# Normalized attention and a gated feed-forward layer: more work open to VectorE, the 1/6 at the end, and another written-out order

## The chip, the cores and the metric

One core of a Trainium2 chip runs the kernel as one program. The metric is the device time in microseconds, 425.38 as the median of three runs of the kernel before.

## The reference

```python
q, k, v: (8, 12, 448, 64)          # batch, heads, sequence, head size, float32
q_n = q / sqrt(mean(q * q) + 1e-6) * g_q;  k_n likewise with g_k
attn = softmax(q_n @ k_n.T / sqrt(64))
x = (attn @ v) as 3584 tokens x 768
h = x @ w_in                        # 768 -> 2048
g = h * clip(h + 3, 0, 6) / 6
out = g @ w_out                     # 2048 -> 768, float32
```

## The kernel before

The work goes by pairs of heads: pair P is batch P // 6 and two of its twelve heads, 48 pairs in all. For a pair, SyncE's queue loads queries, keys and values as tiles of 112 rows (four tokens to a row). Squares (`sq`, for half of a pair's queries `sqh`) are taken on ScalarE or GpSimd, VectorE sums them (`red`), ScalarE makes the inverse root from a logarithm and an exponential (`ln`, `ex`), and a scaling writes bf16 (`sc`, half: `sch`). For pairs 0 to 12 TensorE transposes the scaled tiles, and a copy takes them out of PSUM (`cq` for queries, `ck` for keys, which also multiplies by the gains); from pair 13 on a transposing DMA on SyncE's queue does it (`dt`), and `kt` applies the gains. Values are copied to bf16 (`cv`). Scores (`s`, on 64 of the array's 128 rows, two heads side by side) go to PSUM, ScalarE takes the exponential (`e`), TensorE multiplies with the values (`av`), VectorE divides (`rd`, `xn`), and the result is transposed into `xT`, by TensorE for the first two sequences and by DMA (`dx`) for the others.

The feed-forward part is split into groups: a hidden group (`h`) fills a PSUM bank with six matmuls, then the clamp (`relu`, line 726) and the product with h (`gate`, line 729) take it to `gT`; an output group (`y`) fills a bank with sixteen matmuls, copied out (`cy`) and stored. In the middle of the kernel these groups have two PSUM banks in turn. Attention of one sequence runs interleaved with feed-forward work of the one before it.

The first sequence is worked in halves, and short matmuls on zeros (`warm`, `idle`) fill TensorE in between. The weights come in by eight DMAs from GpSimd's queue.

Nothing of this is scheduled on the chip. `Plan.add` collects 2386 operations with the engines each may run on; `ORDER` is a written-out list of all their numbers in the order in which they are issued, and `WAY` says for an operation which of its allowed engines takes it (0, the first, where it isn't named). Each engine works its part strictly in that order, and so does SyncE's queue of loads, transposing DMAs and stores. Operation 369 is the load of the values of pair 12, 663 and 760 are the transposing DMAs of pairs 13 and 14.

The clamp and gate before:

```python
em(nc.scalar.activation(out=ts[:], in_=ps()[:, 0:S], func=RELU, bias=0.5, scale=1.0 / 6.0))
em(nc.vector.scalar_tensor_tensor(
    out=out, in0=shape(ts[:]), scalar=1.0, in1=shape(ps()[:, 0:S]), op0=A_MIN, op1=A_MULT))
```

Of the kernel before, what the change touches and what calls it, by code (L numbers as in the profile page):

```python
# [12 lines left out]
A_MIN = mybir.AluOpType.min  # L13
LN = mybir.ActivationFunctionType.Ln
# [9 lines left out]
    53: 1, 61: 1, 63: 2, 67: 1, 68: 1, 69: 1, 76: 1, 80: 1, 83: 1, 95: 1, 99: 1, 101: 2, 121: 1, 122: 1,  # L24
    126: 1, 128: 2, 148: 1, 199: 1, 212: 1, 214: 1, 232: 1, 346: 2, 386: 1, 387: 1, 393: 2, 457: 1, 462: 1,
    469: 1, 474: 1, 481: 1, 515: 1, 542: 1, 552: 1, 553: 1, 573: 1, 589: 2, 617: 1, 624: 1, 635: 1, 637: 1,
    646: 1, 653: 2, 664: 1, 672: 1, 737: 1, 738: 1, 769: 1, 770: 1, 776: 2, 795: 1, 802: 2, 854: 1, 926: 1,
    949: 1, 977: 1, 1005: 1, 1075: 1, 1134: 1, 1140: 2, 1160: 1, 1237: 1, 1269: 1, 1285: 1, 1286: 1, 1309:
    1, 1317: 1, 1318: 1, 1344: 1, 1350: 1, 1401: 1, 1408: 2, 1428: 1, 1434: 1, 1497: 1, 1565: 1, 1589: 1,
    1597: 1, 1615: 1, 1630: 2, 1641: 1, 1649: 1, 1673: 1, 1681: 1, 1688: 2, 1699: 1, 1707: 1, 1714: 2, 1725:  # L30
    1, 1785: 1, 1790: 1, 1817: 1, 1822: 1, 1857: 1, 1865: 1, 1872: 1, 1898: 2, 1941: 1, 1964: 1, 1979: 2,
    2039: 1, 2044: 1, 2072: 1, 2095: 1, 2114: 2, 2143: 1, 2151: 1, 2159: 1, 2195: 1, 2245: 1, 2286: 1, 2313:
    1, 2333: 1, 2338: 1, 2345: 1, 2357: 1, 2374: 1,
# [3 lines left out]
    9, 20, 8, 21, 22, 10, 23, 11, 24, 25, 13, 28, 26, 14, 27, 53, 16, 31, 55, 32, 17, 33, 54, 212, 12, 34,  # L37
    56, 213, 57, 29, 69, 92, 58, 61, 59, 19, 60, 35, 68, 73, 62, 36, 91, 30, 37, 74, 70, 214, 84, 66, 64,
    15, 75, 38, 67, 77, 65, 39, 71, 40, 118, 72, 83, 102, 76, 81, 119, 103, 104, 85, 41, 18, 79, 94, 95, 42,
    43, 93, 82, 80, 44, 215, 86, 230, 129, 96, 120, 87, 105, 45, 46, 89, 145, 47, 63, 97, 88, 130, 108, 146,  # L40
    131, 109, 110, 231, 111, 98, 132, 106, 99, 112, 113, 48, 100, 107, 216, 122, 114, 121, 133, 78, 115,
    158, 134, 232, 156, 149, 116, 217, 123, 49, 157, 50, 0, 135, 51, 136, 148, 117, 172, 233, 90, 124, 52,
    150, 125, 137, 159, 138, 127, 139, 164, 165, 126, 234, 140, 151, 235, 162, 152, 173, 174, 141, 154, 163,
    160, 142, 166, 153, 161, 175, 143, 167, 144, 188, 168, 101, 178, 189, 218, 176, 190, 179, 219, 177, 220,
    191, 180, 169, 200, 248, 242, 221, 181, 128, 201, 170, 155, 202, 225, 182, 249, 222, 236, 203, 183, 171,
    368, 223, 303, 184, 250, 192, 185, 245, 193, 304, 305, 339, 224, 186, 238, 194, 306, 187, 239, 315, 227,
    251, 340, 195, 204, 316, 246, 205, 196, 197, 317, 206, 237, 247, 341, 318, 207, 198, 360, 226, 240, 327,
    199, 329, 252, 208, 228, 342, 307, 253, 209, 308, 328, 271, 255, 241, 309, 147, 210, 310, 272, 211, 254,
    330, 243, 311, 347, 312, 273, 359, 319, 229, 320, 343, 256, 348, 321, 322, 257, 349, 323, 344, 313, 324,
    258, 350, 370, 314, 259, 325, 274, 1, 275, 371, 326, 331, 361, 372, 351, 373, 332, 333, 345, 374, 352,  # L50
    334, 375, 353, 362, 354, 335, 363, 397, 386, 355, 336, 364, 376, 263, 356, 398, 264, 377, 357, 337, 365,
    358, 399, 387, 338, 401, 378, 400, 265, 402, 276, 2, 388, 405, 500, 277, 379, 403, 501, 380, 489, 381,
    406, 404, 407, 408, 382, 389, 502, 409, 383, 506, 390, 3, 503, 410, 266, 384, 411, 385, 267, 507, 391,
    268, 412, 278, 504, 508, 505, 490, 512, 283, 513, 509, 346, 510, 392, 535, 491, 511, 284, 366, 514, 269,
    516, 525, 517, 515, 270, 518, 285, 519, 537, 492, 520, 524, 279, 493, 521, 536, 280, 286, 494, 522, 281,
    291, 523, 538, 495, 282, 539, 292, 526, 540, 541, 533, 287, 367, 545, 527, 293, 546, 543, 261, 528, 288,
    542, 544, 530, 260, 294, 547, 289, 548, 395, 566, 583, 549, 564, 290, 567, 299, 497, 550, 300, 529, 394,
    565, 393, 572, 244, 551, 301, 295, 554, 498, 573, 302, 296, 552, 262, 570, 582, 421, 297, 422, 571, 553,
    568, 298, 593, 5, 595, 569, 584, 423, 413, 414, 4, 424, 596, 574, 415, 555, 416, 417, 594, 425, 418,
    575, 576, 419, 577, 556, 426, 420, 557, 601, 585, 427, 559, 599, 578, 429, 602, 428, 430, 558, 579, 607,  # L60
    433, 431, 618, 617, 434, 432, 580, 435, 437, 496, 581, 646, 438, 560, 436, 600, 619, 6, 597, 441, 439,
    647, 605, 598, 608, 442, 606, 440, 630, 7, 443, 628, 603, 445, 444, 604, 648, 446, 586, 738, 609, 588,
    449, 447, 450, 620, 629, 448, 587, 610, 611, 631, 612, 634, 453, 613, 451, 614, 454, 635, 452, 636, 615,
    637, 458, 616, 621, 623, 632, 657, 659, 633, 459, 531, 658, 460, 622, 638, 660, 639, 455, 663, 640, 748,
    750, 749, 461, 591, 456, 532, 649, 751, 462, 561, 641, 470, 650, 642, 562, 651, 643, 664, 471, 625, 457,
    472, 652, 590, 644, 465, 645, 760, 737, 661, 754, 739, 756, 662, 466, 626, 769, 473, 796, 499, 740, 770,
    665, 534, 474, 666, 741, 755, 467, 743, 771, 746, 667, 795, 655, 668, 482, 742, 757, 669, 369, 670, 468,
    654, 821, 761, 671, 483, 786, 469, 672, 822, 772, 797, 780, 773, 782, 752, 781, 484, 396, 774, 823, 753,
    745, 477, 775, 478, 798, 783, 589, 758, 653, 812, 806, 853, 808, 759, 485, 762, 486, 804, 763, 764, 799,
    765, 777, 800, 809, 677, 766, 767, 479, 807, 880, 787, 768, 480, 854, 801, 678, 481, 624, 784, 855, 778,  # L70
    832, 879, 834, 785, 563, 673, 813, 824, 844, 674, 856, 679, 788, 825, 680, 675, 789, 826, 790, 835, 791,
    464, 685, 792, 827, 592, 793, 833, 686, 803, 676, 810, 744, 687, 840, 881, 838, 830, 857, 811, 681, 859,
    747, 682, 688, 861, 1017, 814, 683, 815, 794, 816, 841, 817, 684, 693, 858, 818, 839, 694, 819, 870,
    1018, 845, 866, 695, 836, 864, 867, 689, 696, 1049, 829, 776, 690, 865, 627, 1050, 701, 1019, 691, 820,
    702, 837, 692, 890, 892, 703, 802, 842, 463, 697, 1020, 843, 704, 896, 698, 1051, 882, 846, 699, 847,
    709, 476, 883, 891, 700, 848, 887, 849, 710, 1021, 893, 850, 888, 1023, 871, 705, 711, 851, 706, 884,
    1052, 712, 852, 1028, 707, 1030, 868, 885, 717, 708, 869, 862, 718, 1022, 1075, 872, 1040, 873, 719,
    874, 1031, 713, 720, 875, 1026, 1029, 714, 876, 886, 877, 725, 1076, 715, 878, 1034, 716, 894, 1035,
    726, 1101, 897, 721, 895, 1077, 1025, 828, 722, 727, 1102, 898, 899, 723, 900, 1134, 901, 724, 1133,
    1060, 1078, 1036, 1053, 902, 1061, 729, 903, 1055, 730, 728, 1037, 904, 1041, 1032, 731, 733, 1033, 734,  # L80
    732, 779, 1079, 1062, 1066, 735, 1038, 1081, 1086, 1039, 905, 736, 1103, 906, 1054, 656, 1042, 907,
    1057, 909, 1063, 1159, 908, 1043, 1092, 910, 913, 1024, 911, 1044, 912, 914, 860, 1135, 1045, 915, 917,
    1080, 1087, 918, 1046, 916, 1136, 1124, 919, 1067, 922, 1047, 923, 1058, 1093, 475, 1088, 1064, 1112,
    1084, 1065, 924, 889, 925, 1089, 1048, 1068, 926, 1160, 920, 1104, 1113, 1069, 488, 1070, 1071, 921,
    805, 1114, 1072, 1118, 1137, 1073, 1105, 929, 1115, 1139, 1110, 1161, 930, 1083, 1119, 1107, 933, 1109,
    1125, 931, 934, 831, 1106, 932, 1120, 935, 1090, 1144, 1162, 1318, 937, 936, 1138, 1091, 938, 1056,
    1167, 941, 1285, 942, 1141, 939, 1286, 1094, 863, 940, 1095, 1096, 1317, 1150, 1097, 945, 943, 1098,
    1099, 1163, 1121, 946, 1165, 944, 1142, 947, 1319, 1074, 1164, 950, 1146, 1287, 1116, 1100, 951, 1117,
    952, 1288, 1320, 1145, 1294, 948, 1168, 1147, 953, 949, 1059, 1170, 1289, 954, 1122, 1291, 928, 1172,
    1123, 957, 1027, 958, 1370, 487, 1126, 959, 1127, 1343, 1128, 1171, 1129, 961, 1130, 960, 1290, 962,  # L90
    1131, 965, 963, 1151, 1369, 966, 964, 1148, 967, 1082, 1296, 969, 1149, 968, 1111, 970, 1344, 1176,
# [865 lines left out]
```

## Time and profile before

| | |
|---|---|
| median of 3 runs | 425.38 us (425.29 to 426.16) |
| the profiled execution | 425.55 us, its span 423.8 us |
| TensorE busy | 414.8 us, 98% of the span |
| ScalarE busy | 287.1 us, 68% |
| VectorE busy | 225.8 us, 53% |
| GpSimd busy | 178.1 us, 42% |
| TensorE's granted clock | 0.998 |

The busy time of TensorE counts matmuls whose ends are modelled, so it says where TensorE has work and not that it runs at its peak. The other engines are far from full over the whole span, but not in every stage; the profile has to be read by stages. In the profile's names ACT is ScalarE, DVE VectorE, POOL GpSimd, SP SyncE, PE TensorE; a q behind a name is that engine's issuing queue.

### The profile page before, as it was taken

To read this page: it belongs to the slowest core of one execution; us is meant where nothing else is said; L and a number is where in the kernel's file an instruction comes from. 1 tells how busy PE (TensorE), PEld (TensorE's weight loads), DVE (VectorE), ACT (ScalarE), POOL (GpSimd) and SP (SyncE) were. 2 spreads that over 40 slices of the span, in tenths; PEclk is the share of its full clock that TensorE was granted. 3 is DMA by queue.
4 is the path that set the end of the run, shared out by engine and by line. 5 is a ranking of instruction groups with operands and counts; after the bars stand their busy time and mean duration, and the time that the engine had idled before them with its cause. 6 is when DMAs were issued, how large, how long until landed. Compare 5 with 4: busy or idle time off the path is not lost.

```text
span 423.8 us, 9991 instructions
## 1 busy us (share of the span) xinstructions
PE 414.8 (98%) x3960; PEld 243.0 (57%) x3960; DVE 225.8 (53%) x453; ACT 287.1 (68%) x523; POOL 178.1 (42%) x206
## 2 busy tenths in 40 slices
PE   7999999989999999999999999999999999999996
PEld 3566877645555555555555555555555555555564
DVE  5988774769775476565445455543453433232310
ACT  6999988789987768787767867666846662133101
POOL 3999685678774462593035655333030200000000
PEclk9999999999999999999999999999999999999999
DMA  7999999999869958595768469273144202200323
GB/s 249 292 282 220 244 216 170 274 267 274 207 155 267 249 129 226 172 197 144 198 154 239 110 159 215 79 184 77 40 106 112 57 26 60 43 7 0 109 68 118
DMA packets 98931, 67.77 MB, mean 160 GB/s; under 512 B 53156, under 2 KB 95428, under 8 KB 98884
## 3 DMA queue, kind: packets, MB, share of 16 engines
q1 hardware_dynamic: 93248, 60.50, 54.6%
q0 software_dynamic: 5248, 6.29, 9.0%
q8 instruction: 31, 0.51, 0.5%
q10 hardware_dynamic: 388, 0.34, 0.3%
q14 instruction: 16, 0.13, 0.1%
HBM read 50.23 MB, written 11.01 MB: 145 GB/s over the span
## 4 chain that ended last, share of the span: by engine, by line
PE 84%; DMA 6%; ACT 4%; issue 1%; DVE 1%; SPq 1%; POOL 1%; DVEq 0%; POOLq 0%; ACTq 0%
PE M L767 28%; PE M L789 27%; PE X L675 9%; PE S L589 5%; PE S L789 5%; PE X L589 3%; PE M L748 3%; DMA qk<-in_q_dram 3%; ACT eT L617 3%; DMA w_in_sb<-in_moe_w_in_dram 2%; DMA vf<-in_v_dram 1%; PE X L767 1%; PE S L767 1%; POOL qks L367 1%; PE X L789 1%
## 5 line engine op out<-in xcount | busy, mean ns | idle before, releaser
L367 POOL TENSOR_TENSOR qks<-qk,rs 112x512 bf16<-112x512 f32 (+1 forms) x88 | 88.9, 1024 | 119.5 <-ACT rs L428 94.8
L789 PE MATMUL M<-w_out_sb,gT 128*128 128x384 bf16 x752 | 138.0, 326 | 0.0
L767 PE MATMUL M<-xT,w_in_sb 128*128 128x448 bf16 x618 | 134.0, 353 | 0.0
L789 PEld LDWEIGHTS <-gT 128*128 128x128 bf16 x912 | 84.2, 98 | 58.3 <-issue 7.3
L729 DVE SCALAR_TENSOR_TENSOR gT<-ts,M 128x448 bf16<-128x448 f32 x119 | 73.3, 616 | 74.5 <-ACT ts L726 74.3
L595 ACT ACTIVATE eT<-S 112x896 bf16<-112x896 f32 x112 | 99.7, 916 | 6.9 <-PE X L675 3.6
L726 ACT ACTIVATE ts<-M 128x448 f32<-128x448 f32 x119 | 64.9, 546 | 46.5 <-PE M L767 39.4
L767 PEld LDWEIGHTS <-w_in_sb 128*128 128x128 bf16 x672 | 60.3, 98 | 58.2 <-issue 11.9
L364 POOL TENSOR_TENSOR sq<-qk 112x512 f32<-112x512 f32 (+1 forms) x59 | 59.1, 1012 | 24.1 <-DMA qk<-in_q_dram 9.6
L595 ACT ACTIVATE eT<-X 112x896 bf16<-112x896 f32 x56 | 51.3, 917 | 20.2 <-PE X L589 19.2
L675 PEld LDWEIGHTS <-eT 112*128 112x128 bf16 x1344 | 52.3, 97 | 15.1 <-DVE va L346 1.5
L675 PE MATMUL X<-va,eT 112*128 112x65 bf16 x1344 | 55.3, 193 | 1.4 <-DVE va L346 1.1
L449 DVE TENSOR_REDUCE ssq<-sq 112x16 f32<-112x1024 f32 x42 | 50.7, 1212 | 7.1 <-ACT sq L362 3.8
L589 PE MATMUL S<-T 64*128 64x448 bf16 x224 | 34.1, 353 | 0.1
L350 DVE COPY y<-M 128x384 f32<-128x384 f32 x23 | 12.8, 557 | 39.1 <-PE M L789 39.1
L694 DVE TENSOR_TENSOR xn<-X,rd 112x512 bf16<-112x512 f32 x42 | 28.9, 689 | 2.1 <-DMA xT<-xn 1.3
L691 DVE RECIPROCAL rd<-X 112x8 f32<-112x8 f32 x42 | 8.7, 207 | 38.2 <-PE X L675 35.4
L589 PEld LDWEIGHTS <-T 64*128 64x128 bf16 x336 | 12.3, 94 | 24.0 <-issue 18.8
L362 ACT ACTIVATE sq<-qk 112x512 f32<-112x512 f32 (+1 forms) x38 | 22.2, 595 | 5.6 <-DMA qk<-in_q_dram 3.4
L348 ACT COPY y<-M 128x384 f32<-128x384 f32 x24 | 11.5, 480 | 19.0 <-PE M L789 18.7
L748 PE MATMUL M<-xT,w_in_sb 128*128 128x224 bf16 x192 | 23.1, 259 | 0.2 <-DMA w_in_sb<-in_moe_w_in_dram 0.2
L789 PE MATMUL S<-w_out_sb,gT 128*128 128x384 bf16 (+1 forms) x128 | 22.3, 316 | 0.0
(88 smaller groups left out, 303.1 us busy)
## 6 DMA issues: line engine op xcount, KB each, us to landing
qk<-in_k_dram SPq DMA_DIRECT2D x45, 256.0 KB, 4.2
qk<-in_q_dram SPq DMA_DIRECT2D x45, 256.0 KB, 4.0
vf<-in_v_dram SPq DMA_DIRECT2D x45, 256.0 KB, 4.3
w_in_sb<-in_moe_w_in_dram POOLq DMA_DIRECT2D x4, 768.0 KB, 8.5
w_out_sb<-in_moe_w_out_dram POOLq DMA_DIRECT2D x4, 768.0 KB, 9.2
out_dram<-y SPq DMA_DIRECT2D x7, 336.0 KB, 3.9
out_dram<-y SPq DMA_DIRECT2D x8, 288.0 KB, 3.5
out_dram<-y SPq DMA_DIRECT2D x8, 240.0 KB, 2.7
```

The source lines that it names most:

```text
L364: em(nc.gpsimd.tensor_tensor(out=out, in0=in_, in1=in_, op=A_MULT))
L367: em((nc.vector if e == DVE else nc.gpsimd).tensor_tensor(out=out, in0=in_, in1=by.unsqueeze(3).to_broadcast(list(in_.shape)), op=A_MULT))
L449: em(nc.vector.tensor_reduce(out=ssq[:].rearrange("p i n -> p (i n)"), in_=sq[:].rearrange("p i (n d) -> p (i n) d", d=D), axis=AX_X, op=A ...
L589: em(nc.tensor.matmul(out=ps[:, a, 0:S], lhsT=qkT[r, S + t * TP:S + t * TP + 128], rhs=qkT[r, 0:S], start=True, stop=True))
L595: em(nc.scalar.activation(out=eT[:, t, 0:S2].rearrange("p (a s) -> p a s", a=2), in_=ps[0:TP, :, 0:S], func=EXP, bias=0.0, scale=1.0))
L675: em(nc.tensor.matmul(out=X_ps[:, a, i * E1:(i + 1) * E1], lhsT=eT[:, t, c:c + 128], rhs=va[:, a, t, :], start=(t == 0 and i == 0), stop=( ...
L694: em(nc.vector.tensor_tensor(out=xn[:].rearrange("p i a d -> p a i d"), in0=view()[:, :, :, 0:D], in1=rd[:].unsqueeze(3).to_broadcast([TP, ...
L726: em(nc.scalar.activation(out=ts[:], in_=ps()[:, 0:S], func=RELU, bias=0.5, scale=1.0 / 6.0))
L729: em(nc.vector.scalar_tensor_tensor(out=out, in0=shape(ts[:]), scalar=1.0, in1=shape(ps()[:, 0:S]), op0=A_MIN, op1=A_MULT))
L748: em(nc.tensor.matmul(out=ps()[:, f * SH:(f + 1) * SH], lhsT=w_in_sb[:, kt, f0:f0 + 128], rhs=xT[:, kt, z * SH:(z + 1) * SH], start=(kt == ...
L767: em(nc.tensor.matmul(out=ps()[:, 0:S], lhsT=w_in_sb[:, kt, f * 128:(f + 1) * 128], rhs=xT[:, kt, :], start=(kt == 0), stop=(kt == NKT - 1)))
L789: em(nc.tensor.matmul(out=ps()[:, 0:nc0], lhsT=gT[:, f, i * 128:(i + 1) * 128], rhs=w_out_sb[:, f, c0:c0 + nc0], start=(f == 0), stop=(f = ...
```

## The change

It has five parts. Squares may go to VectorE too for pairs below 15 (`NVE`), and scalings likewise. The clamp may go to VectorE for the first two sequences; to make that one instruction of two operations, ReLU(h + 3) is stored instead of ReLU(h/6 + 1/2), the gate clips at 6 instead of 1, and the missing 1/6 is applied in the copies of y. Value loads of the last three pairs are issued as two halves (`NSL`). `ORDER` and `WAY` are replaced altogether; the operations keep their numbers and what they depend on.

By engine, the new `WAY` moves 19 of the 128 clamps to VectorE; squares go from 57 on GpSimd and 33 on ScalarE to 48, 40 and 2 on VectorE; scalings from 4 on VectorE to 7, and one half scaling; value copies from 26 on GpSimd, 17 on VectorE, 5 on ScalarE to 18, 14 and 16; `kt` from 22 on VectorE and 13 on ScalarE to 20 and 15.

```diff
+    NSL = 3
+    NVE = 15
...
     def square(e, out, in_):
         if e == ACT:
             em(nc.scalar.square(out=out, in_=in_))
         else:
-            em(nc.gpsimd.tensor_tensor(out=out, in0=in_, in1=in_, op=A_MULT))
+            em((nc.vector if e == DVE else nc.gpsimd).tensor_tensor(out=out, in0=in_, in1=in_, op=A_MULT))
...
+            split = i == 2 and P >= NP - NSL
...
-                em(nc.sync.dma_start(out=dst, in_=rows))
+                for h in ((0, 1) if split else (slice(0, 2),)):
+                    em(nc.sync.dma_start(out=dst[:, h], in_=rows[:, h]))
...
-            plan.add("sq", [POOL, ACT], f_sq, ...
+            plan.add("sq", [POOL, ACT, DVE] if P < NVE else [POOL, ACT], f_sq, ...
...
-            plan.add("sc", [POOL], f_sc, ...
+            plan.add("sc", [POOL, DVE] if P < NVE else [POOL], f_sc, ...
...
-        def f_r(_):
-            em(nc.scalar.activation(out=ts[:], in_=ps()[:, 0:S], func=RELU, bias=0.5, scale=1.0 / 6.0))
+        def f_r(e):
+            if e == DVE:
+                em(nc.vector.tensor_scalar(ts[:], ps()[:, 0:S], 3.0, 0.0, A_ADD, A_MAX))
+            else:
+                em(nc.scalar.activation(out=ts[:], in_=ps()[:, 0:S], func=RELU, bias=3.0, scale=1.0))
...
-                out=out, in0=shape(ts[:]), scalar=1.0, in1=shape(ps()[:, 0:S]), op0=A_MIN, op1=A_MULT))
-        plan.add("relu", [ACT], f_r, [res], [("ts", key)])
+                out=out, in0=shape(ts[:]), scalar=6.0, in1=shape(ps()[:, 0:S]), op0=A_MIN, op1=A_MULT))
+        plan.add("relu", [ACT, DVE] if b < 2 else [ACT], f_r, [res], [("ts", key)])
...
-                copy(e, ys[:, c0:c0 + nc0], ps()[:, 0:nc0])
+                o, y = ys[:, c0:c0 + nc0], ps()[:, 0:nc0]
+                if e == ACT:
+                    em(nc.scalar.activation(out=o, in_=y, func=COPY, bias=0.0, scale=1.0 / 6.0))
+                else:
+                    em(nc.vector.tensor_scalar(o, y, 1.0 / 6.0, None, A_MULT))
```

The start of SyncE's queue behind operation 663 (k16: keys of pair 16; dt: transposing DMA of `T`), before and after:

```
before  dt(13) k17 q15 q16 k16 q18 q17 dt(14) k18 v14 v15 k20 k19 v12 q19 dt(15) v13 q20 dt(16)
after   dt(13) k16 v13 v15 q16 q17 k19 k17 k18 v12 k21 q19 q18 dt(14) q20 k20 v17 dt(15) v14 dt(16)
```

More of the change, by code (lines that the diff above doesn't have):

```diff
@@ L13 @@
 A_MIN = mybir.AluOpType.min
+A_MAX = mybir.AluOpType.max
 LN = mybir.ActivationFunctionType.Ln
@@ L415, in load, with fn @@
             dst = dst[0:np] if i == 2 else dst[0:np, i]
-            def fn(_, dst=dst, src=src, np=np):
+            split = i == 2 and P >= NP - NSL
+            def fn(_, dst=dst, src=src, np=np, split=split):
                 rows = src[b, hs].rearrange("h (p t) d -> p h (t d)", t=T)
                 rows = bass.AP(rows.tensor, rows.offset, [[rows.ap[0][0], np]] + [list(d) for d in rows.ap[1:]])
-                em(nc.sync.dma_start(out=dst, in_=rows))
+                for h in ((0, 1) if split else (slice(0, 2),)):
+                    em(nc.sync.dma_start(out=dst[:, h], in_=rows[:, h]))
             plan.add("ld", [SP], fn, (), [res] if i == 2 else [(*res, 1)] if i else [(*res, 0, z) for z in range(2)])
@@ L444, in f_sq @@
                 square(e, sq[:, i], qk[0:TP, i].rearrange("p h x -> p (h x)"))
-            plan.add("sq", [POOL, ACT], f_sq, [(*qr, 1)] if i else [(*qr, 0, z) for z in range(2)],
+            plan.add("sq", [POOL, ACT, DVE] if P < NVE else [POOL, ACT], f_sq, [(*qr, 1)] if i else [(*qr, 0, z) for z in range(2)],
                      [("sq", P % NSQ, 2)] if i else [("sq", P % NSQ, z) for z in range(2)])
@@ L459, in f_sc @@
                       qk[0:TP, i].rearrange("p h (t d) -> p h t d", d=D), rs[:, i].rearrange("p (h t) -> p h t", h=2))
-            plan.add("sc", [POOL], f_sc, ([(*qr, 1)] if i else [(*qr, 0, z) for z in range(2)]) + [wr[i]],
+            plan.add("sc", [POOL, DVE] if P < NVE else [POOL], f_sc, ([(*qr, 1)] if i else [(*qr, 0, z) for z in range(2)]) + [wr[i]],
                      [("qks", P % NQS, 2)] if i else [("qks", P % NQS, z) for z in range(2)])
@@ L469, in f_sq @@
                    qk[0:TP, 0, :, z * 2 * D:(z + 1) * 2 * D])
-        plan.add("sqh", [POOL, ACT], f_sq, [(*qr, 0, z)], [("sq", P % NSQ, z)])
+        plan.add("sqh", [POOL, ACT, DVE], f_sq, [(*qr, 0, z)], [("sq", P % NSQ, z)])
     def half_scale(P, z, rs, rr):
@@ L494, in f_sq @@
             square(e, sq[:, 8 * D:], qk[0:TP, 1].rearrange("p h x -> p (h x)"))
-        plan.add("sq", [POOL, ACT], f_sq, [(*qr, 1)], [("sq", P % NSQ, 2)])
+        plan.add("sq", [POOL, ACT, DVE], f_sq, [(*qr, 1)], [("sq", P % NSQ, 2)])
         half_square(P, 0)
```

281 rows, old and new, of tables (ORDER, WAY) are left out of this document.

## The prediction

> **What bounds the kernel now.** I read the busy time of each engine by stage first, then who waited for whom, then the chain of waits, and the single instructions last. By stage (columns: window, length, then busy us and count for matmul, weight load, VectorE, ScalarE, GpSimd, then TensorE's clock, DMA share, GB/s):
>
> ```profile
> 10.00:20.00 10.00, 9.18 (x124) 5.11 (x126) 9.68 (x25) 9.94 (x26) 8.55 (x12) 1.00 1.07 307
> 20.00:35.00 15.00, 14.55 (x261) 10.25 (x260) 12.70 (x42) 14.84 (x26) 14.21 (x19) 1.00 1.00 276
> 35.00:45.00 10.00, 9.58 (x140) 7.25 (x139) 7.93 (x18) 9.41 (x17) 9.88 (x12) 1.00 1.20 196
> ...
> 60.00:92.00 32.00, 30.92 (x341) 20.38 (x340) 19.46 (x36) 25.54 (x46) 20.39 (x23) 1.00 1.06 229
> 92.00:250.00 158.00, 158.00 (x1510) 87.41 (x1509) 95.24 (x174) 125.59 (x231) 84.39 (x91) 1.00 0.75 193
> 250.00:360.00 110.00, 110.00 (x1007) 61.86 (x1003) 48.49 (x96) 69.44 (x114) 27.33 (x29) 1.00 0.43 101
> ```
>
> From 92 to 360 us TensorE is never idle: no faster work elsewhere can be felt there. The set of TensorE's instructions is the same in both programs, so what can change is its idle time, nearly all before 92 us, and the price of its transitions. From 10 to 35 us ScalarE is the full one (9.94 of 10, 14.84 of 15), with VectorE (9.68) close behind. The waits of TensorE, in the first 45 us and from 45 to 360:
>
> ```profile
> PE M L537 <- POOL qks L367: 1.0, 1, 1.0
> ```
> ```profile
> PE X L675 <- DVE va L346: 1.1, 1, 1.1
> PE X L675 <- ACT eT L595: 0.3, 1, 0.3
> ```
>
> The one large wait behind the front is the 1.1 us for a copy of values. The chain of waits (start, us, what) tells whose it is:
>
> ```profile
> 75.98 2.06 POOL qks L367 x2
> ...
> 78.05 1.23 SPq L556
> ...
> 82.44 6.31 DMA vf<-in_v_dram
> ...
> 89.47 0.10 DVE va L346
> 89.57 0.05 issue
> 89.61 1.15 PE X L675 x32
> ```
>
> Two scalings on GpSimd release the transposing DMA of pair 14 (operation 760); it stands at the head of SyncE's queue, and behind it five loads and then the values of pair 12 (operation 369), issued at 82.44, landed 6.31 us later. VectorE copies them, and TensorE has waited.
>
> **The change, part by part.** *The value load, -1.1 us.* In the changed order operation 369 stands ahead of 760, eight loads behind the transposing DMA of pair 13 (operation 663), whose issue before was
>
> ```profile
> 72.75 1.34 SPq L556 DMA_TRANSPOSE T<-qks  x1
> ```
>
> Between 78.05 and 82.44 one transposing DMA and five loads took 1.23 us and 3.16 us, 0.63 each. With the same start: 72.75 + 1.34 + 8 x 0.63 = 79.1 us issued, with 6.31 to land 85.4, some 3 us before TensorE asks (89.61 - 1.1 = 88.5). The wait goes; what is late next behind it is a load whose place is new as well (a rival, below). Bounds: 1.1 gained, or nothing.
>
> *Score batches, -0.6 us.* Scores use half the rows of the array. The chain shows what entering and leaving them costs:
>
> ```profile
> 93.20 0.29 PE X L589 x2
> 93.49 0.38 PE S L589 x4
> 93.87 1.24 PE M L767 x6
> 95.11 0.97 PE X L675 x32
> 96.09 1.14 PE M L767 x6
> ```
>
> The first pair takes 0.29 us where each of the next two takes 0.19, and six matmuls behind scores take 1.24 where six others take 1.14: 0.2 us per batch. I counted unbroken batches in both built programs: 90 before, 87 after. 3 x 0.2 = 0.6 us, on TensorE itself.
>
> *The front, +0.5 us.* Single instructions of ScalarE, then one of GpSimd (start, us, what, idle before it):
>
> ```profile
> 6.88 0.42 ACT L362 ACTIVATE sq<-qk 112x256 f32<-112x256 f32 x1 [1.55 <-DMA qk<-in_q_dram]
> ...
> 9.35 0.62 ACT L362 ACTIVATE sq<-qk 112x512 f32<-112x512 f32 x1
> 9.87 0.90 ACT L617 ACTIVATE eT<-S 112x896 bf16<-112x896 f32 x1
> ...
> 10.97 0.62 ACT L356 ACTIVATE gT<-M,gp_t 128x448 bf16<-128x448 bf16 x1
> ```
> ```profile
> 10.66 1.04 POOL L364 TENSOR_TENSOR sq<-qk 112x512 f32<-112x512 f32 x1 [1.06 <-DMA qk<-in_k_dram]
> ```
>
> The third load lands at about 6.86, the eighth at about 10.6: 0.75 us each. The changed program squares the first keys on VectorE, but ScalarE's queue then holds, ahead of the copy of the scaled keys of pair 0, the squares of the third, fourth and fifth loads. The fifth lands at 6.86 + 2 x 0.75 = 8.4. Then a square (the next one starts 0.52 later: 9.35 to 9.87), the copy of the keys (row at 10.97; now ScalarE's, VectorE's before; 0.5 until the next starts), three short steps for roots and a half copy, some 0.7, its end and the scores, 0.5: the first exponential starts at about 10.6 us, not 9.87. That is 0.7 later on the engine that is full until 35 us. ScalarE's work from there to 35 us stays the same within a tenth: by the two orders a half square, a key copy and a half copy leave it, a whole square and a value copy come. VectorE's order in the first 35 us gains a square, a value copy, a half scaling, two copies and a whole scaling and loses a scaling, a value copy and a copy, about 1.1 us more in a stage in which it was 9.68 of 10 busy. Its free time of 2.3 us from 20 to 35 us can take that. Bounds: 0 (TensorE's fillers and ScalarE's 0.8 us free between 10 and 45 us take it up) and +1.8 (0.7 + 1.1, all passed on). I take 0.5, near the delay that ScalarE's rows give.
>
> *Clamps, 0.* Of 128, 19 move to VectorE, all before 121 us. Nothing before shows a clamp there; the nearest rows (mean ns last but one):
>
> ```profile
> L726 ACT ACTIVATE ts<-M 128x448 f32<-128x448 f32 x119 | 64.9, 546 | 46.5 <-PE M L767 39.4
> ```
> ```profile
> L729 DVE SCALAR_TENSOR_TENSOR gT<-ts,M 128x448 bf16<-128x448 f32 x119 | 73.3, 616 | 74.5 <-ACT ts L726 74.3
> L449 DVE TENSOR_REDUCE ssq<-sq 112x16 f32<-112x1024 f32 x42 | 50.7, 1212 | 7.1 <-ACT sq L362 3.8 <-POOL sq L364 3.3
> ...
> L367 DVE TENSOR_TENSOR qks<-qk,rs 112x512 bf16<-112x512 f32 x4 | 2.7, 687 | 0.2
> ```
>
> I take the gate's 616 ns, the same size from the same memory: 0.07 us more for each bank, and 19 x 0.62 = 11.8 us of work moved from ScalarE to VectorE, which has 12.5 us free from 60 to 92. ScalarE gets value copies and squares in exchange, so little is freed. What hides it is the other bank's group of six matmuls (1.14) with attention between; without that cover it is the first rival.
>
> *Squares and scalings, 0.* Two squares, three whole scalings more and a half one go to VectorE (687 ns for a scaling). They have a price on GpSimd:
>
> ```profile
> 13.97 1.06 POOL L367 TENSOR_TENSOR qks<-qk,rs 112x256 bf16<-112x256 f32 x1
> ```
> ```profile
> 13.87 0.69 DVE L367 TENSOR_TENSOR qks<-qk,rs 112x512 bf16<-112x512 f32 x1
> ```
> ```profile
> L367 POOL TENSOR_TENSOR qks<-qk,late_rs 112x256 bf16<-112x256 f32 x5 | 3.0, 613 | 0.0
> ```
>
> A half scaling that took 1.06 us on GpSimd instead of 0.61 began 0.1 us into a scaling on VectorE: 0.45 lost. Six more such instructions cost GpSimd up to 2.7 us. I count it as nothing, since GpSimd hands over nine squares and eight value copies. The Trainium skill ("SBUF — State Buffer", section "Who interferes with whom") says that a VectorE instruction with two SBUF inputs and a GpSimd one that reads SBUF exclude each other, and that the one issued first keeps the ports to its end; the row agrees, and by that rule VectorE can also be the one that waits. With 0.45 for each of the three in the first 40 us on the path, the sum would be 1.35 us higher.
>
> *The rest, 0.* The 1/6 in the copies of y replaces a copy by a scaling copy of the same size. The bounds are a tenth of a microsecond each way for one copy, off the path except for the last, after which the same store follows: the end is as long as it was. The split value loads of the last three pairs add three issues where TensorE waits for nothing (250 to 360 us).
>
> The profiled execution took 425.55 us: 425.55 - 1.1 - 0.6 + 0.5 = 424.35. The median of the runs is 425.38, 0.17 lower: **424.2 us**. About 0.2% (0.85 us) is what a measurement of this kernel can tell from no change.
>
> **The rivals.** *VectorE becomes the bound with the clamps (slower).* Clamp and gate now stand in one queue with the reductions of 1.21 us. A bank takes 2 x 0.62 = 1.24 us to empty, and 2.45 if a reduction is ahead; the other bank covers 1.14, attention in between about half a microsecond: 0.8 us of wait. It decides from the point where several clamps meet a reduction. Four of the 19 make 3.2 us: 424.2 + 3.2 = 427.4. For it: VectorE is 7.9 of 10 busy from 35 to 45 us, and the clamps between there and 60 us come on top. Against it: 12.5 us free from 60 to 92.
>
> *Another wait of a microsecond in place of the one removed (no change).* Every load has a new place, and one that lands late as pair 12's values did gives 424.2 + 1.1 = 425.3; the front at its full +1.8, or the ports' 1.35, gives 425.5 or 425.6. For it: DMA shares of about 1 until 92 us, and the values of pair 14 now behind one transposing DMA more. Against it: those of pairs 12, 13 and 15 stand earlier.
>
> *The front gets shorter (faster).* TensorE's idle time from 10 to 45 us is 0.82 + 0.45 + 0.42 = 1.7 us, and with the pair-0 queries scaled sooner the 1.0 us wait for GpSimd at 8.4 us goes. Without the 0.5 and with 1.0 less: 422.7.
>
> That the change does less than it says is built in: few instructions move, the order is what differs.
>
> **How the numbers follow.** Forecast 0.42, shorter front 0.10, another wait 0.20, VectorE bound 0.28. Faster is the first two, 0.52; same 0.20; slower 0.28. The forecast's own range is 423.7 (front at 0) to 424.7 (0.5 more). The range for all runs from 422.7 to the slow rival's 427.4; beyond lie a still shorter front and more than four clamps caught, under 2 in 10.
>
> **What would show it.** Right: no wait of TensorE for the value copies near 88 us, the first exponential at about 10.6 us, TensorE without idle time from 92 to 360 us. Wrong: waits of TensorE for VectorE's gate between 45 and 120 us (the slower rival), a new wait for a DMA, or a first exponential before 9.9 us.

## The result, and the profile after

The changed kernel takes 424.32 us as the median of 22 runs (422.91 to 425.56); the kernel before, run beside it, 425.78 us (22 runs, 423.86 to 427.79). The ratio is 0.9967 with a 95% interval of 0.9954 to 0.998: 1.4 us faster. The forecast was 424.2. The profiled execution took 424.31 us with a span of 422.5; that of before 425.55 and 423.8.

The stages after (columns as in the prediction):

```profile
10.00:20.00 10.00, 8.41 (x122) 5.40 (x123) 9.92 (x28) 9.97 (x25) 8.65 (x13) 1.00 1.10 333
20.00:35.00 15.00, 13.81 (x252) 9.91 (x252) 11.75 (x39) 13.80 (x25) 12.35 (x17) 1.00 1.03 267
...
60.00:92.00 32.00, 32.00 (x348) 20.81 (x346) 23.02 (x41) 25.16 (x48) 18.95 (x20) 1.00 1.11 242
92.00:250.00 158.00, 157.85 (x1516) 88.00 (x1514) 99.98 (x178) 127.11 (x229) 77.77 (x82) 1.00 0.82 194
250.00:360.00 110.00, 110.00 (x995) 62.04 (x994) 50.81 (x99) 70.35 (x117) 24.25 (x26) 1.00 0.42 93
```

From 60 to 92 us TensorE is now without idle time (32.00; before 30.92). In the front it has more: it works 8.41 us from 10 to 20 us against 9.18, and 13.81 from 20 to 35 us against 14.55. Over the first 92 us the idle time is 5.3 us in both profiles, so this pair alone does not show that the change won anything there; the runs have to. TensorE's waits after, the whole span:

```profile
PE XF L643 <- DVE xT L356: 0.9, 1, 0.9
PE S L621 <- ACT gT L354: 0.7, 1, 0.7
...
PE M L546 <- POOL qks L373: 0.4, 1, 0.4
PE M L760 <- DVE gT L741: 0.3, 1, 0.3
```

The wait for the values of pair 12 (1.1 us before) is gone, and so is that of 1.0 us for GpSimd's scaling at 8.4 us. Two of the front have come instead: 0.9 us for a copy of `xT`, and 0.7 us, at 9.48 us, for ScalarE's copy of half of pair 0's queries (`gT`, line 354). The only wait for a gate listed is 0.3 us, at 57.8 us, so the slower rival did not come. The load itself, in SyncE's queue, then VectorE's copy of it and TensorE's use (start, us, what):

```profile
72.70 1.35 SPq L565 DMA_TRANSPOSE T<-qks  x1
...
78.31 0.46 SPq L429 DMA_DIRECT2D vf<-in_v_dram  x1
```
```profile
85.41 0.68 DVE L352 TENSOR_SCALAR_CACHE_REDUCE va<-vf 112x512 bf16<-112x512 f32 x1
```
```profile
88.26 1.14 PE L684 MATMUL X<-va,eT 112*128 112x65 bf16 x32
```

It is issued at 78.31 (79.1 by the prediction) and copied from 85.41 to 86.09 with no wait ahead of the copy; TensorE asks 2.9 us after the copy's start (by the prediction, 3 us after the landing).

The end is a surprise. The last copy of y and the span, before, after, and in the run named below that has only the changed program text:

```profile
core 0 of [0], span 423.8 us
...
420.12 0.32 ACT L348 COPY y<-X 128x192 f32<-128x192 f32 x1 [2.16 <-PE X L789]
```
```profile
core 0 of [0], span 422.5 us
...
419.39 0.33 ACT L812 ACTIVATE y<-X 128x192 f32<-128x192 f32 x1 [2.00 <-DMA out_dram<-y]
```
```profile
core 0 of [0], span 424.8 us
...
421.68 0.33 ACT L809 ACTIVATE y<-X 128x192 f32<-128x192 f32 x1 [2.15 <-PE X L798]
```

From the end of that copy to the end of the span it is 423.8 - 420.44 = 3.4 us before, and 2.8 us in the other two. Of the 1.3 us by which the two profiled spans differ, 0.7 come before the last copy and 0.6 after it.

### The profile page after: what moved, and what is told of

Same layout as the page of the kernel before. It is cut to its first block, busy times and chain, and to the rows that moved or that the text cites. A ratio compares the mean times of both kernels' runs of the same rounds, so it can differ in the third digit from the quotient of the medians.

```text
span 422.5 us, 9972 instructions
## 1 busy us (share of the span) xinstructions
PE 413.9 (98%) x3959; PEld 244.5 (58%) x3960; DVE 237.3 (56%) x468; ACT 288.6 (68%) x523; POOL 161.6 (38%) x186
## 4 chain that ended last, share of the span: by engine, by line
PE 82%; ACT 6%; DVE 4%; DMA 4%; issue 1%; SPq 1%; POOL 0%; ACTq 0%; DVEq 0%; POOLq 0%
PE M L801 29%; PE M L779 26%; PE X L684 9%; PE S L598 5%; ACT eT L626 4%; PE S L801 4%; PE M L760 3%; PE X L598 3%; PE X L779 1%; DMA qk<-in_q_dram 1%; DMA out_dram<-y 1%; DVE ssq L458 1%; DMA qk<-in_k_dram 1%; PE S L779 1%; DVE gT L741 1%
## 5 line engine op out<-in xcount | busy, mean ns | idle before, releaser
L373 POOL TENSOR_TENSOR qks<-qk,rs 112x512 bf16<-112x512 f32 (+1 forms) x85 | 86.4, 1033 | 114.7 <-ACT rs L437 77.1
L738 ACT ACTIVATE ts<-M 128x448 f32<-128x448 f32 x100 | 54.6, 546 | 42.1 <-PE M L779 28.4
L370 POOL TENSOR_TENSOR sq<-qk 112x512 f32<-112x512 f32 (+1 forms) x52 | 51.3, 993 | 52.9 <-DMA qk<-in_q_dram 31.5
L814 DVE TENSOR_SCALAR y<-M 128x384 f32<-128x384 f32 x24 | 13.4, 556 | 30.6 <-PE M L801 30.5
L368 ACT ACTIVATE sq<-qk 112x512 f32<-112x512 f32 (+1 forms) x43 | 25.7, 609 | 3.2 <-DMA qk<-in_q_dram 2.7
L812 ACT ACTIVATE y<-M 128x384 f32<-128x384 f32 x23 | 11.3, 491 | 20.0 <-PE M L801 18.4
```

Of the source, the lines that this page charges most:

```text
L370: em((nc.vector if e == DVE else nc.gpsimd).tensor_tensor(out=out, in0=in_, in1=in_, op=A_MULT))
L373: em((nc.vector if e == DVE else nc.gpsimd).tensor_tensor(out=out, in0=in_, in1=by.unsqueeze(3).to_broadcast(list(in_.shape)), op=A_MULT))
```

## The experiments

Runs of one program lie 2 to 6 us apart, so medians are compared, of 12 runs (4 and 5 for the split batches and the clamps, whose runs lie closer). The 95% interval of a ratio reaches about 0.2% (0.7 to 1.0 us) to each side, and the difference of two runs is less certain still. The ratio given is not that of the two medians: the two differ by up to 0.4 us, and where a reading hangs on it both are named. Each group of runs had its own runs of the kernel before beside it: medians 425.67, 425.78 and 425.63.

**The kernel before, a second profile.**

> The kernel before once more, for a second profile of it. If the 1.1 us wait for the value copy of pair 12 belongs to its order, it is there again, near 89 us and between 0.8 and 1.5 us long. If it was an accident of one execution, it is gone. What follows the last matmul took 3.7 us before and 3.1 after the change: if that differs by chance from execution to execution, this one can lie anywhere from 3.0 to 4.0 us; if it belongs to the order, it is 3.7 again.

425.23 us, span 423.5. The wait that the prediction sized at 1.1 us was 0.2 us in this execution, far below the 0.8 that I expected at least, and others of 0.5 us stood elsewhere:

```profile
PE X L675 <- ACT eT L595: 0.5, 1, 0.5
```

VectorE's copy of these values ended only 0.3 us earlier than in the first profile (89.25 us against 89.56); TensorE came to it 0.6 us later (89.09 against 88.53). So the wait shrank mostly because TensorE itself was later. The profile shows which wait is there, but a single execution does not show its mean size. The end was again 3.4 us.

**The load of pair 12 alone, in the kernel before.**

```diff
+ORDER.remove(369)
+ORDER.insert(ORDER.index(760), 369)
```

> The order before, with one operation moved: the load of the values of pair 12 stands ahead of the transposing DMA of pair 14, as in the changed order. Theory (the load behind the transposing DMA is the wait): the 1.1 us wait is gone, the time falls by about 1.1 us (ratio 0.9974). Rival (the load is only one of several that are late there, another wait follows at once): the wait moves to another operation within the next 10 us and the time falls by less than 0.4 us (ratio 0.999 or more).

423.87 us, ratio 0.9964 (0.9947 to 0.9981): 1.8 us faster by the medians, 1.5 by the ratio, against the 1.1 of the theory. The wait for the value copy is not in its profile. Its end is 2.9 us, although the program text is that of before but for the moved load; 0.4 us of the gain is this shorter end.

**The same load put back late in the changed kernel.**

```diff
+ORDER.remove(369)
+ORDER.insert(ORDER.index(760) + 1, 369)
```

> The changed order, with the load of the values of pair 12 put behind the transposing DMA of pair 14 again. Theory: TensorE waits again, and since VectorE's copy now stands earlier in its queue than before, with product and copies out behind it, by more than 1.1 us: issued near 83 us, landed near 89, the wait of TensorE 1.8 us or up to 4 with what VectorE holds up; ratio 1.004 to 1.009. Rival (other parts of the new order hide a late load): no wait above 0.5 us, ratio within 0.001 of 1 against the changed kernel.

425.14 us, ratio 0.9987 (0.9969 to 1.0006): 0.8 us slower than the changed kernel, at the edge of what these medians can tell. The wait is back, but at 0.3 us in the profiled execution, and the 1.8 us or more that I expected did not come:

```profile
PE X L686 <- DVE va L354: 0.3, 1, 0.3
```

**The keys of pair 7 loaded earlier in the changed kernel.** The new 0.9 us wait of the first profile is for a copy of `xT` that stands behind a reduction of 1.22 us on VectorE, itself late because the keys of pair 7 (operation 225) were late:

```profile
31.05 1.22 DVE L458 TENSOR_REDUCE ssq<-sq 112x16 f32<-112x1024 f32 x1 [0.98 <-POOL sq L370]
32.19 0.27 DVE L356 COPY xT<-XF 128x224 bf16<-128x224 bf16 x1
```

```diff
+ORDER.remove(225)
+ORDER.insert(ORDER.index(242), 225)      # three loads earlier
```

> The changed order, with the load of the keys of pair 7 moved three places forward in SyncE's queue, ahead of the queries of pair 9. In the changed kernel it lands at 29.9 us, the square on GpSimd begins at once, VectorE waits for it with a reduction (31.05 to 32.27), and a copy of xT stands behind, for which TensorE waits 0.9 us. Theory (this load is where the front lost its time): the reduction comes some 0.9 us earlier, the 0.9 us wait shrinks below 0.2, pair 6's last half of scores and all behind it 0.7 us or more earlier, and the time falls by 0.5 to 0.9 us against the changed kernel. Rival (ScalarE, full in the front, is the bound): the wait goes and TensorE waits for an exponential instead, the time within 0.3 us of the changed kernel.

423.72 us, ratio 0.996 (0.9943 to 0.9977). The wait for `xT` is gone, but 1.5 us for the copy of half of pair 0's queries stand in the same front, and 0.6 us below the changed kernel is inside what these medians can tell. The last run below did not repeat it.

**Twenty score batches split.**

```diff
+AHEAD = [(m, s), ...]      # 20 pairs: the operation after a batch, the batch's last scores
+for m, s in AHEAD:
+    ORDER.remove(m)
+    ORDER.insert(ORDER.index(s), m)
```

> The changed kernel with twenty batches of three score operations, all behind 92 us, split in two plus one: the feed-forward operation that followed the batch is issued ahead of its last score operation. TensorE's instructions are the same, only their order differs. My theory (each batch costs 0.2 us on TensorE itself, for going to 64 rows and back): 20 x 0.2 = 4.0 us more, 428.3 us against 424.3 for the changed kernel. Rival (the price is only in the first pair's 0.10 us, the 0.10 behind it is the order of other matmuls): 2.0 us more, 426.3. Rival (the records are modelled ends, no real time): 424.3, no change. A wait of ScalarE for a later score would show as idle time of TensorE behind 92 us; I expect none.

432.57 us, ratio 1.0151 (1.0129 to 1.0173): 8.2 us slower than the changed kernel, twice the 4.0 of my theory. One batch in the changed kernel, then the same one split:

```profile
196.67 0.36 PE L598 MATMUL S<-T 64*128 64x448 bf16 x2
...
197.06 0.35 PE L598 MATMUL S<-T 64*128 64x448 bf16 x2
197.34 1.88 PE L779 MATMUL M<-xT,w_in_sb 128*128 128x448 bf16 x9
```
```profile
196.84 0.36 PE L621 MATMUL S<-T 64*128 64x448 bf16 x2
...
197.32 0.74 PE L802 MATMUL M<-xT,w_in_sb 128*128 128x448 bf16 x3
198.00 0.36 PE L621 MATMUL S<-T 64*128 64x448 bf16 x2
198.29 1.31 PE L802 MATMUL M<-xT,w_in_sb 128*128 128x448 bf16 x6
```

From the first scores to the first matmul behind all of it, taken for each of the twenty in both traces, the split batch takes 0.21 us longer in sixteen of them, and 0.36 to 0.77 in the other four. So the price of a transition was right: 20 x 0.21 = 4.2 us. What I had not expected is waiting: the later scores made the exponentials late, and TensorE's waits for them, none behind 92 us in the changed kernel, are

```profile
PE X L707 <- ACT eT L627: 1.4, 5, 0.3
PE S L621 <- ACT eT L627: 0.4, 1, 0.4
```

Its idle time from 92 to 360 us is 2.7 us in all. Some 1.3 us of the 8.2 stay unassigned.

**All 19 clamps back on ScalarE.**

```diff
+for i in (269, 285, 293, 301, ...):      # the 19 clamps that WAY gives to VectorE
+    del WAY[i]
```

> The changed kernel with all 19 clamps back on ScalarE; nothing else moves. My theory (clamps are off the path on either engine): within 0.5 us of the changed kernel, 423.8 to 424.8. Rival (clamps on VectorE delay the emptying of banks): faster without them, by 0.8 us for each clamp that was caught, 423.5 or less. Rival on the other side (the clamps freed ScalarE in a full stage, and the change lives from that): 19 x 0.55 = 10.4 us come back to ScalarE between 35 and 121 us, and a tenth of that on the path makes 425.3 or more.

428.18 us, ratio 1.0056 (1.0038 to 1.0074): 3.9 us slower than the changed kernel. My theory said no change and fell; the rival by which the change lives from the freed ScalarE, 425.3 or more, has the direction right. TensorE waits for gates (the whole span):

```profile
PE M L781 <- DVE gT L743: 2.4, 4, 0.7
PE M L762 <- DVE gT L743: 0.4, 1, 0.4
```

One of these, with VectorE's gate that it waits for and ScalarE's clamp ahead of that:

```profile
98.98 1.30 PE L781 MATMUL M<-xT,w_in_sb 128*128 128x448 bf16 x6 [0.72 <-DVE gT L743]
```
```profile
98.31 1.16 DVE L743 SCALAR_TENSOR_TENSOR gT<-ts,M 128x448 bf16<-128x448 f32 x2 [0.78 <-ACT ts L740]
```
```profile
96.95 0.90 ACT L606 ACTIVATE eT<-S 112x896 bf16<-112x896 f32 x1
97.74 0.54 ACT L740 ACTIVATE ts<-M 128x448 f32<-128x448 f32 x1
```

The clamp stands behind an exponential, the gate behind the clamp, the bank's next matmuls behind the gate. In the changed kernel VectorE does that clamp and goes straight on:

```profile
95.89 0.61 DVE L736 TENSOR_SCALAR ts<-M 128x448 f32<-128x448 f32 x1
96.54 1.15 DVE L741 SCALAR_TENSOR_TENSOR gT<-ts,M 128x448 bf16<-128x448 f32 x2
```

This prices the clamps inside the new order, which counts on them; the old order, without any, had no such waits.

**The changed program text with the old order.** `ORDER` and `WAY` are those of before; the 1/6 in the copies, the clip at 6 and the split loads stay.

> The changed program text with the order and the choice of engines of before: the 1/6 in the copies of y, the clip at 6, the split value loads of the last three pairs are the changed ones; no clamp, square or scaling moves. My theory (all the gain is in the order): 425.7 us, as before, within 0.4. Rival (the end itself is shorter by 0.6 us, from the last copies or the split loads): 425.1, with 2.8 us from the end of the last copy to the end of the span instead of 3.4.

425.2 us, ratio 0.9977 (0.9961 to 0.9994): by the medians 0.6 us faster than before, as much as the end is shorter (the third fence on the end, above), by the ratio 1.0. The rival holds in time and in the end's 2.8 us. That the changed text is the reason is shown for a part only: in the kernel before with one load moved, without this text, 0.4 of the 0.6 us were gone as well.

**Squares and scalings back where they were.**

```diff
+WAY[53] = 1                                   # ScalarE
+for i in (127, 345, 525, 622, 623, 651):      # GpSimd
+    del WAY[i]
```

> The changed kernel with its squares and scalings put back where they ran before: the square of the first keys on ScalarE; one square, three whole scalings, one later one and a half one on GpSimd instead of VectorE. My theory (they are off the path on VectorE, and cost GpSimd little): 424.3, within 0.5. Rival (VectorE and GpSimd exclude each other at the ports, three times 0.45 us on the path in the front): faster without, 423.0. Rival on the other side (GpSimd's queue in the front is the tight one, 14.2 of 15 us busy from 20 to 35 us): each of these takes 1.04 to 1.2 us there, two of them in the front on the path make 426.4.

425.61 us, ratio 1.0002 (0.9977 to 1.0026), with runs from 423.72 to 430.0, the widest spread of all. 423.0, which the ports' exclusion on the path would give, lies outside the interval (424.8 to 426.9), and no single run reached it. The median is 1.3 us above the changed kernel, more than the 0.5 of my theory; but six of these twelve runs show a granted clock of 0.991 to 0.996, as only one of the changed kernel's 22 has, and the other six (0.999 or 1.0) have a median of 424.48, level with it. So a gain from having them on VectorE is not shown.

**The changed kernel again.**

> The changed kernel once more, as a measure beside the others and for a second profile of the same program. My theory: 424.3 us, within 0.4; the first exponential starts 2.2 us after the fifth load lands (7.69 and 9.89 in the first profile), wherever that landing falls between 7.6 and 8.4; TensorE idle for less than 0.4 us from 92 to 360 us. Rival (the front is slower by what the first profile showed, a copy of xT that waits 0.9 us behind a reduction): that wait is there again at 0.9. If it is not, it belonged to that execution's load times and not to the order.

424.32 us, ratio 0.9965 (0.9944 to 0.9986). The wait for `xT` was 0.5 us here, not 0.9, the one for the copy of half of pair 0's queries 1.1, not 0.7, and 0.7 us stood between 60 and 92 us for the weights of the output groups. TensorE was idle for 0.15 us from 92 to 360 us, as in the first profile. ScalarE's square of the fifth load, which waits for it, and its first exponential, in the first profile and in the slowest front of the same order (the run with split batches):

```profile
7.71 0.63 ACT L368 ACTIVATE sq<-qk 112x512 f32<-112x512 f32 x1 [0.34 <-DMA qk<-in_k_dram]
...
9.89 1.73 ACT L626 ACTIVATE eT<-S 112x896 bf16<-112x896 f32 x2
```
```profile
8.35 0.63 ACT L391 ACTIVATE sq<-qk 112x512 f32<-112x512 f32 x1 [0.34 <-DMA qk<-in_k_dram]
...
10.53 1.73 ACT L649 ACTIVATE eT<-S 112x896 bf16<-112x896 f32 x2
```

9.89 - 7.71 and 10.53 - 8.35 are both 2.18 us. In this second profile of the changed kernel it is 10.03 - 7.85, 2.18 again.

**The changed text, the old order and the one load.**

```diff
+ORDER.remove(369)                             # on the text with the old order
+ORDER.insert(ORDER.index(760), 369)
```

> The changed program text with the order of before, and the values of pair 12 (operation 369) moved ahead of the transposing DMA of pair 14 (760). My theory (the order is worth that one load and the score batches): 425.2 - 1.1 = 424.1 us, 0.2 to 0.6 below the changed kernel plus its 0.6 for batches, so level with it. Rival (the load is worth what it measured alone in the kernel before, 1.8): 423.4, which would beat the changed kernel by 0.9 and mean that the rest of its order costs something. Rival (it brought nothing of its own, and other waits set the time): 425.2.

424.2 us, ratio 0.9971 (0.9949 to 0.9992): level with the changed kernel, as my theory had it, and 1.0 us below the same text without the move, by the medians. By the two ratios it is only 0.3.

**Two batches fewer, with the keys of pair 7 early.**

```diff
+ORDER.remove(225)
+ORDER.insert(ORDER.index(242), 225)
+for s, after in ((1062, 1060), (1088, 1086)):
+    ORDER.remove(s)
+    ORDER.insert(ORDER.index(after) + 1, s)
```

> The changed kernel with the keys of pair 7 loaded earlier, as in the run with that change alone (423.7 us), and two single score operations joined to the batch ahead of them, so two batches fewer. My theory (0.21 us a batch, the step that sixteen of the twenty split batches showed): 423.7 - 0.4 = 423.3 us. Rival (the earlier scores wait for an exponential to free their bank): 0.3 to 0.6 us of idle time between 115 and 125 us, and 423.7 to 424.

424.43 us, ratio 0.997 (0.9946 to 0.9994): no gain on the changed kernel. A wait for an exponential appears:

```profile
PE S L603 <- ACT eT L609: 0.5, 1, 0.5
```

which is the rival's mechanism and takes as much as the two batches could bring (0.4 us). Since this kernel has the earlier keys too, their 0.6 us is not established.

No run beat the changed kernel by more than these medians can tell; the lowest were the earlier keys (423.72) and the single moved load in the kernel before (423.87).

## Why the prediction was right, point by point

**The value load, -1.1: right.** Place, cause and cure are shown. Three pairs of runs price it by their medians: 0.8 (put back late), 1.0 (moved in the changed text) and 1.8 (moved in the kernel before, of which 0.4 is the shorter end that its profile shows); by the ratios 0.9, 0.3 and 1.5. Only the last is well clear of the noise, so a gain is shown and its size is known to about 1 us. The size from one profile was luck to a degree: it was 0.2 in a second profile of the kernel before and 0.3 in the kernel with the load put back.

**Score batches, -0.6: the price right, the sum not shown.** A transition costs 0.21 us. But by the count only one of the three batches that went lies in the work behind the front; two are half-width batches of the front, where TensorE waits anyway. TensorE's busy time fell by 0.8 us (414.75 to 413.91), fillers and the front included, and 0.2 us is what this term can claim on the path. What the step left out: with two S banks, where a batch stands also decides when an exponential can start. Splitting cost twice its transitions, and joining gained nothing.

**The front, +0.5: the step right, its input too late.** The chain from the fifth load to the first exponential was put at 10.6 - 8.4 = 2.2 us and measured 2.2 in every profile looked at. The load landed between 7.7 and 8.35 instead of at 8.4: the third load, from which the prediction counted, landed at 6.86 in the profile of before and at 6.20 after, and the two behind it 0.73 and 0.76 us apart, as forecast. So the exponential starts at 9.9 to 10.5. In the profiled pair there was no delay (9.89 against 9.87); over all profiles it starts at 9.47 to 9.87 in the order of before (five) and at 9.89 to 10.53 in the new one and its variants (eight), 0.5 us later on average. TensorE felt this chain as the wait for the half copy of queries at its end, 0.7 us, in place of the 1.0 us for GpSimd's scaling (0.4 in the second profile of before), which the rival of a shorter front had rightly seen go. It lost 0.9 us more at 32 us, behind the late keys of pair 7 (0.5 in the second profile). A gain or a loss of the front in time, as a mean over executions, is not settled.

**Clamps, 0: right for the whole change, wrong in its reason.** One bank waits on VectorE, for 0.3 us, and the slower rival's 3.2 us did not come. "Little is freed" holds for ScalarE's busy time (287.1 us before, 288.6 after). What the reason left out is that the new order has filled the clamps' place on ScalarE with other work: in this order the clamps there cost 3.9 us.

**Squares and scalings, 0: the exclusion is not on the path.** The row of before with 1.06 us for a half scaling instead of 0.61 agrees with what the Trainium skill ("SBUF — State Buffer", section "Who interferes with whom") says; 1.35 us from it on the path would have made the changed kernel slower than its version with these back on GpSimd, and it is not (424.32 against 425.61, or against 424.48 in its six runs with a clock of 0.999 or 1.0).

**The rest, 0: wrong by 0.6.** "The end is as long as it was" failed: the end went from 3.4 to 2.8 us, and the program with the changed text alone is 0.6 us faster by the medians. The forecast did not look behind the last store.

*The signs.* Of the three signs of being right one came as said: no wait for the value copies. TensorE's idle time from 92 to 360 us was 0.15 us and not nothing, and the first exponential stood at 9.89 us, a hair below the 9.9 that was to show the forecast wrong.

In sum: about -1.0 (the load) and -0.6 (the end) are what the runs show, each with the uncertainty said above, and together they are about the 1.4 us. The forecast's two other terms, -0.6 for the batches and +0.5 for the front, leave about nothing between them. So the total was right by the load, and by luck in the rest: the 0.6 of the end, which it did not forecast, is as large as the 0.6 for the batches, which is not shown.

## What to carry to other kernels

In a kernel whose main engine is full, look for the one queue entry that a large wait hangs on: moving a single load did, as far as these medians tell, what a new order of all 2386 operations did. An order written out by hand belongs to its assignment of engines, so undoing one part prices that part inside the order and not by itself. Take the size of a wait for a load from several executions, not from one.

## What was not expected of the hardware

- The same program's runs spread over 4 us (423.59 to 427.3 in one group of 29 runs of the kernel before), with TensorE's granted clock at 0.998 to 1.0; in another group one run took 429.9 us, at 0.996. A load's landing varied by 0.6 us in the front (7.7 to 8.35 for the fifth), and waits for loads varied as well (1.1 and 0.2 us for the values of pair 12 in two profiles of the kernel before).
- The time behind the last copy is 3.4 us in both profiles of the kernel before, 2.9 in that kernel with one load moved, and 2.8 in all others looked at. The copy and the issue of the last store are alike (0.32 and 0.38 us before, 0.33 and 0.37 after), so the difference lies behind them. By the sequencers' records in the traces the last store lands 1.82 to 1.83 us after the last copy in the kernel before, in that with one load moved, in the changed text with the old order and in the changed kernel. Then SyncE's closing waits end 0.39 us later in the first two and 0.21 to 0.22 later in the others; and GpSimd's next step comes after 0.36 us in the kernel before, after 0.06 to 0.07 in the other three. The first part goes with the changed text, the second does not; why either differs stays open.
